# Attention followed by a squared-ReLU layer: score and value work grouped by three pairs of heads instead of two

## The chip, the cores and the metric

The kernel runs on one core of a Trainium2 chip. The time is the device time of one execution in microseconds; the kernel before takes 417.61 us (median of 3 runs, 417.29 to 417.97). The engines of the core are TensorE (PE; its weight loads are listed apart as PEld), VectorE (DVE), ScalarE (ACT), GpSimd (POOL) and SyncE (SP). TensorE reads the on-chip memory SBUF and writes the accumulator memory PSUM; DVE and ACT empty PSUM.

## What is computed

Attention with one added to the softmax's denominator, over 8 batches, 12 heads, 448 positions and a head size of 64; then two matrix products with a squared ReLU between them, over the 3584 rows of the attention's output.

```python
batch, n_heads, seq, head_dim = (8, 12, 448, 64)     # q, k, v in float32
n_tokens, d_model, d_ff = (3584, 768, 2048)          # w_in: 768x2048, w_out: 2048x768

scores = scale * np.matmul(q, k.transpose(0, 1, 3, 2))
m = np.max(scores, axis=-1, keepdims=True)
e = np.exp(scores - m)
attn = e / (np.sum(e, axis=-1, keepdims=True) + np.exp(-m) + 1e-09)
attn_out = np.matmul(attn, v)
# x: attn_out with the heads side by side, (3584, 768)
h = x @ w_in                                         # "first product"
r = np.maximum(h, 0.0)
g = r * r
out = g @ w_out                                      # "second product"
```

The kernel computes e as exp of the scaled scores and the denominator as their sum plus one, which is the same quotient.

## The kernel before

Heads are taken in pairs: 6 pairs per batch. A *unit* is one pair's scores, exponentials (`et`), their row sums and its values. Batch 0 is cut into 192 and 256 query positions, so units 0 to 11 are batch 0, 12 to 17 batch 1, and units 18 to 53 (batches 2 to 7, 36 pairs) form the main loop. Batches 0 to 2 are turned by TensorE from naturally laid out loads (`qn`, `kn`); batches 3 to 7 are turned by transposing DMAs from a float16 copy in memory.

A half-unit of scores is eight matmuls (four for batches 0 to 2) on 64 rows of the array each, two at a time in two row tiles. ACT empties each PSUM buffer with the exponential; there are two such buffers. DVE adds the four chunks of `et` to one (`es`), in three steps:

```python
    def scores(u, et, c):
        b, pr, q0, n = u
        qk = qks[b]
        two = [] if n == S else s_psum.tile([P, 2, 512], FP32, name="sp")
        for kk in (2 * c, 2 * c + 1):
            sp = s_psum.tile([P, 2, 512], FP32, name="sp") if n == S else two
            # ... [batches 0 to 2: one matmul of n columns per head; others:]
                for h in range(2):
                    for odd in range(2):
                        r = slice(64 * odd, 64 * odd + 64)
                        # ... [x, kx, which: where q and k of this half lie]
                        nc.tensor.matmul(sp[:, odd, h * (S // 2):(h + 1) * (S // 2)],
                                         qk[r, which, kx:kx + 2 * P - 1:2], qk[r, 0, x:x + S // 2],
                                         start=True, stop=True)
            if n == S:
                exp(chunk(et, u, c, kk).rearrange("p (o x) -> p o x", o=2), sp[:, :, 0:S])
    # ...

    def add_chunks(u, et, es, half, step):
        n = u[3]
        if n == S:
            e = et.rearrange("p (k x) -> p k x", k=RUN)
            if step < 2:
                nc.vector.tensor_add((es, half[:, 0:2 * S])[step], e[:, 2 * step], e[:, 2 * step + 1])
            else:
                nc.vector.tensor_add(es, es, half[:, 0:2 * S])
        # ...
```

Values, the row sums and the first product use the array in two column tiles of 64. A row sum is a matmul with ones, followed on ACT by Ln and by Exp of its negative, which gives the reciprocal; DVE multiplies the values with it:

```python
    def values(u, et, xp, o=0):
        b, pr, _, n = u
        for kk in range(RUN):
            for h in range(2):
                nc.tensor.matmul(xp[64 * h:64 * h + 64, o:o + n], vns[b][:, 2 * pr + h, kk, :],
                                 of_head(chunk(et, u, kk // 2, kk), u, h), start=(kk == 0), stop=(kk == RUN - 1))

    def row_sums(us, sums):

        zp = mp_tile()
        # ... [for each unit u, of n columns, and its es:]
                for h in range(2):
                    nc.tensor.matmul(zp[64 * h:64 * h + 64, j * n:(j + 1) * n], ones, of_head(total, u, h),
                                     start=(x == 0), stop=(x == len(parts) - 1))
        rcp = z_pool.tile([128, 512], FP32, name="rcp")
        nc.scalar.activation(out=rcp[:, 0:m], in_=zp[:, 0:m], func=AF.Ln, bias=one_b)
        nc.scalar.activation(out=rcp[:, 0:m], in_=rcp[:, 0:m], func=AF.Exp, scale=-1.0)
        return rcp

    def normalise(us, xp, rcp):
        b, pr, q0, n = us[0]
        # ... [two units at once in batch 0]
        nc.vector.tensor_mul(xts[b][:, pr, q0:q0 + n], xp[:, 0:n], rcp[:, 0:n])

    joined = [-1]

    def mp_tile(dtype=FP32):
        if joined[0] >= 0:
            joined[0] += 1
        pool, name = (x_psum, "xp") if joined[0] > 0 and joined[0] % 4 == 0 else (m_psum, "mp")
        return pool.tile([128, 512] if dtype == FP32 else [128, 2, 512], dtype, name=name)
```

`mp_tile` gives the PSUM tiles of everything but the scores. From the main loop on (`joined`), its tiles go around four buffers: three of `m_psum` (`mp`) and, every fourth time, the one of `x_psum` (`xp`).

The first product runs tile by tile (twelve matmuls of 64 output rows for 448 positions), each emptied by DVE with a maximum and a square into `gs`. The second product has a form in column tiles, one with the whole array, and one in row tiles, which splits the contraction over two PSUM tiles (`op`, `lo`) that are added on emptying:

```python
    def product(out_, lhsT, rhs, start, stop):

        if mode[0] == COLS2:
            for x in (0, 64):
                nc.tensor.matmul(out_[x:x + 64], lhsT[:, x:x + 64], rhs, start=start, stop=stop)
        else:
            nc.tensor.matmul(out_, lhsT, rhs, start=start, stop=stop)

    def tile_in(t0, n, f0, per):

        xt, x0 = xts[t0 // S], t0 % S
        m = per * n
        hp = mp_tile()
        for j in range(per):
            fb = f0 + j
            for dc in range(DCH):
                product(hp[:, j * n:(j + 1) * n], win[:, dc, fb * 128:(fb + 1) * 128],
                        xt[:, dc, x0:x0 + n], start=(dc == 0), stop=(dc == DCH - 1))
                if j < per - 1 or dc < DCH - 1:
                    yield n / 2.4
        rt = r_pool.tile([128, 512], FP16, name="rt")
        nc.vector.tensor_scalar(out=rt[:, 0:m], in0=hp[:, 0:m], scalar1=0.0, scalar2=None, op0=ALU.max)
        r = rt[:, 0:m].rearrange("p (j n) -> p j n", j=per)
        nc.vector.tensor_mul(gs[:, f0:f0 + per, t0 % RING:t0 % RING + n], r, r)
        yield n / 2.4
    # ...
    def tile_out(tok, n0, w):

        if n0 == 0:
            ots[tok] = osb_pool.tile([128, DM], FP32, name="ot")
        ot = ots[tok]
        rows = mode[0] == ROWS2
        op = mp_tile()
        lo = mp_tile() if rows else None
        for fb in range(NFFB):
            g = gs[:, fb, tok % RING:tok % RING + 128]
            if rows:
                for x, o in ((0, op), (64, lo)):
                    nc.tensor.matmul(o[:, 0:w], g[x:x + 64], wout[x:x + 64, fb, n0:n0 + w],
                                     start=(fb == 0), stop=(fb == NFFB - 1))
            else:
                product(op[:, 0:w], g, wout[:, fb, n0:n0 + w], start=(fb == 0), stop=(fb == NFFB - 1))
            if fb < NFFB - 1:
                yield w / 2.4
        if rows and n0 == 0:
            nc.vector.tensor_scalar(out=ot[:, n0:n0 + w], in0=op[:, 0:w], scalar1=OUT_SCALE, scalar2=None, op0=ALU.mult)
        else:
            nc.scalar.activation(out=ot[:, n0:n0 + w], in_=op[:, 0:w], func=AF.Copy, scale=OUT_SCALE)
        if rows:
            nc.vector.scalar_tensor_tensor(out=ot[:, n0:n0 + w], in0=lo[:, 0:w], scalar=OUT_SCALE,
                                           in1=ot[:, n0:n0 + w], op0=ALU.mult, op1=ALU.add)
        # ... [store]
```

Work is kept in two queues, `ins` (first product) and `outs` (second product). In units 0 to 17 the first product of batch 0 is dealt out between the scores and values of batches 0 and 1 by `share`. In the main loop, second product in row tiles stands between the scores, and the first product of the batch before stands after the values:

```python
    for i in range(2 * NPAIR, 3 * NPAIR):
        u, et, es, half = begin(i)
        prev = units[i - 1]
        first = i == 2 * NPAIR
        if not first:
            xp = x_psum.tile([128, 512], FP32, name="xp")
        mode[0] = COLS2
        scores(u, et, 0)
        if i in transpose_at:
            transposes(*transpose_at[i])
        # ... [loads]
        drain(left() * 0.5 if first else share[0] * 0.45)
        scores(u, et, 1)
        if first:
            # ... [the last two units of batch 0]
        else:
            done = [prev]
            rcp = row_sums(done, (ess.pop(i - 1)[0:1],))
            values(prev, ets.pop(i - 1), xp)
        drain(share[0] * 0.15)
        for step in range(3):
            add_chunks(u, et, es, half, step)
            drain(share[0] * (0.15, 0.1, 0.15)[step])
        if i == 3 * NPAIR - 1 and ins and ins[0][0] < ins[0][1]:
            run(ins)
        normalise(done, xp, rcp)
        if first:
            queue(FIRST, S - FIRST)
            share[0] = left() / (NPAIR + 1.5)

    pending = [3 * NPAIR - 1]
    joined[0] = 0
    complete(S)
    # ...
    def rows(n):
        mode[0] = ROWS2
        while outs and n > 0:
            one(outs)
            n -= 1
        mode[0] = COLS2

    for c in range((NU - 3 * NPAIR) // 2):
        i = 3 * NPAIR + 2 * c
        b, pr = units[i][0:2]
        new = []
        for j in range(2):
            new.append(begin(i + j))
        (ua, ea, sa, ha), (ub, eb, sb, hb) = new
        scores(ua, ea, 0)
        rows(11)
        scores(ua, ea, 1)
        add_chunks(ua, ea, sa, ha, 0)
        rows(11)
        scores(ub, eb, 0)
        add_chunks(ua, ea, sa, ha, 1)
        add_chunks(ua, ea, sa, ha, 2)
        rows(10)
        scores(ub, eb, 1)
        add_chunks(ub, eb, sb, hb, 0)
        mode[0] = COLS2
        for at in pending:
            if at not in rcps:
                rcps[at] = row_sums([units[at]], (ess.pop(at)[0:1],))
            xp = mp_tile()
            values(units[at], ets.pop(at), xp)
            normalise([units[at]], xp, rcps.pop(at))
        add_chunks(ub, eb, sb, hb, 1)
        add_chunks(ub, eb, sb, hb, 2)
        if b in ON_PE and pr + 2 < NPAIR:
            transposes(b, pr + 2)
            transposes(b, pr + 3)
        if pr == 0:
            run(ins, len(ins))
            queue((b - 1) * S, S)
            if b > 2:
                run(outs)
            # ... [loads of the next batches]

        n, early = ((3, 0 if b > 2 else 1), (7, 3), (6, 3))[pr // 2]
        run(ins, early)
        for at in (i, i + 1):
            rcps[at] = row_sums([units[at]], (ess.pop(at)[0:1],))
        run(ins, n - early)
        if pr == NPAIR - 2:
            complete(b * S)
        pending = [i, i + 1]
    # ... [values of the last round, then the rest of both products with the whole array]
```

Of the kernel before, what the change touches and what calls it, by code (L numbers as in the profile page):

```python
# [9 lines left out]
FP16 = mybir.dt.float16  # L10
# [5 lines left out]
def kernel(  # L16
# [11 lines left out]
    B, H, S, D = q.shape  # L28
# [5 lines left out]
    RUN = 4  # L34
# [15 lines left out]
    qk_pool = ctx.enter_context(tc.tile_pool(name="qk", bufs=2))  # L50
    e_pool = ctx.enter_context(tc.tile_pool(name="e", bufs=4))
    es_pool = ctx.enter_context(tc.tile_pool(name="es", bufs=2))
    z_pool = ctx.enter_context(tc.tile_pool(name="z", bufs=2))
    r_pool = ctx.enter_context(tc.tile_pool(name="r", bufs=2))
    osb_pool = ctx.enter_context(tc.tile_pool(name="osb", bufs=2))

# [26 lines left out]
    def load_natural(b, p0, p1):  # L83

        raw = b == 0 and p1 <= 3
        for n, r in (("q", q_r), ("k", k_r)):
            src = r[b, :, 2 * p0:2 * p1]
            if raw:
                if p0 == 0:
                    whole[n] = e_pool.tile([P, RUN * S], FP32, name="et")  # L90
                t = whole[n][:, p0 * 512:(p0 + 1) * 512].rearrange("p (h t d) -> p h t d", h=2, t=RUN)
                (nc.sync if n == "q" else nc.scalar).dma_start(out=t, in_=src)
            else:
                if p0 % 3 == 0:
                    whole[n] = nat.tile([P, NPAIR, RUN, D], FP16, name=f"{n}n{p0 // 3}")
                t = whole[n][:, 2 * (p0 % 3):2 * (p0 % 3 + p1 - p0)]
                nc.gpsimd.dma_start(out=t, in_=src)
            for pr in range(p0, p1):
                naturals[n, b, pr] = t[:, 2 * (pr - p0):2 * (pr - p0) + 2]
# [292 lines left out]
    def left():  # L392
        return sum(t[0] for t in ins)
# [23 lines left out]
    transpose_at = {pr - 1: (0, pr) for pr in range(1, NPAIR)}  # L417
    for pr in range(NPAIR):
        transpose_at[NPAIR + 3 + pr] = (1, pr)
    transpose_at[16], transpose_at[17] = (2, 0), (2, 1)  # L420

    def keep_warm(n):
        wp = m_psum.tile([128, 512], FP32, name="mp")
# [11 lines left out]
        nc.gpsimd.tensor_copy(last_of, qks[b][0:1, :, 0:1])  # L435

    def begin(i):
        ets[i] = e_pool.tile([P, RUN * 2 * S], FP16, name="et")
        es = es_pool.tile([P, 2 * S], FP16, name=f"es{i % 2}")
        half = es_pool.tile([P, 1024], FP16, name="half")  # L440
        ess[i] = (es, half)
        return units[i], ets[i], es, half
# [8 lines left out]
    for i in range(2 * NPAIR):  # L451
# [8 lines left out]
        if i == NPAIR:  # L460
            values(units[i - 1], ets.pop(i - 1), xp, units[i - 1][3])
            rcp = row_sums(two, (ess.pop(i - 2)[0:1], ess.pop(i - 1)[0:1]))
            normalise(two, xp, rcp)
            queue(0, FIRST)
            share[0] = left() / (NPAIR + 2)
        if i in transpose_at:
            transposes(*transpose_at[i])
        if i == 0:
# [26 lines left out]
    for i in range(2 * NPAIR, 3 * NPAIR):  # L495
# [9 lines left out]
        if i == 2 * NPAIR + 2:  # L505
# [2 lines left out]
                load_wout(HALF, j, 2)  # L508
            load_v(2, 0, 6)
            stage(3)  # L510
        drain(left() * 0.5 if first else share[0] * 0.45)
        scores(u, et, 1)
        if first:
            done = units[i - 2:i]
# [7 lines left out]
        for step in range(3):  # L522
            add_chunks(u, et, es, half, step)
            drain(share[0] * (0.15, 0.1, 0.15)[step])
        if i == 3 * NPAIR - 1 and ins and ins[0][0] < ins[0][1]:
            run(ins)
        normalise(done, xp, rcp)
        if first:
            queue(FIRST, S - FIRST)
            share[0] = left() / (NPAIR + 1.5)  # L530

# [8 lines left out]
            n -= 1  # L542
        mode[0] = COLS2

    for c in range((NU - 3 * NPAIR) // 2):
        i = 3 * NPAIR + 2 * c
        b, pr = units[i][0:2]
        new = []
        for j in range(2):
            new.append(begin(i + j))  # L550
        (ua, ea, sa, ha), (ub, eb, sb, hb) = new
        scores(ua, ea, 0)
        rows(11)
        scores(ua, ea, 1)
        add_chunks(ua, ea, sa, ha, 0)
        rows(11)
        scores(ub, eb, 0)
        add_chunks(ua, ea, sa, ha, 1)
        add_chunks(ua, ea, sa, ha, 2)
        rows(10)  # L560
        scores(ub, eb, 1)
        add_chunks(ub, eb, sb, hb, 0)
        mode[0] = COLS2
        for at in pending:
            if at not in rcps:
                rcps[at] = row_sums([units[at]], (ess.pop(at)[0:1],))
            xp = mp_tile()
            values(units[at], ets.pop(at), xp)
            normalise([units[at]], xp, rcps.pop(at))
        add_chunks(ub, eb, sb, hb, 1)  # L570
        add_chunks(ub, eb, sb, hb, 2)
        if b in ON_PE and pr + 2 < NPAIR:
            transposes(b, pr + 2)
            transposes(b, pr + 3)
        if pr == 0:
            run(ins, len(ins))
            queue((b - 1) * S, S)
            if b > 2:
                run(outs)
            if b + 1 < B:  # L580
                transposed_loads(b + 1)
                hold(b + 1)
                load_v(b + 1, 0, NPAIR)
                if b + 2 < B:
                    stage(b + 2)

        n, early = ((3, 0 if b > 2 else 1), (7, 3), (6, 3))[pr // 2]
        run(ins, early)
        for at in (i, i + 1):
            rcps[at] = row_sums([units[at]], (ess.pop(at)[0:1],))  # L590
        run(ins, n - early)
        if pr == NPAIR - 2:
            complete(b * S)
        pending = [i, i + 1]
    for at in pending:
        xp = mp_tile()
        values(units[at], ets.pop(at), xp)
        normalise([units[at]], xp, rcps.pop(at))
    mode[0] = FULL
    run(outs, 3)  # L600
    queue((B - 1) * S, S)
# [31 lines left out]
```

The softmax here doesn't subtract the row's maximum and nothing guards it: scores larger than these inputs give would overflow.

## Time and profile before

| kernel before | |
|---|---|
| time, median of 3 | 417.61 us (417.29 to 417.97) |
| span of the profiled execution | 415.9 us, granted TensorE clock 1.000 |
| PE busy | 405.5 us, 98% of the span, 4721 matmuls |
| DVE busy | 278.8 us, 67% |
| ACT busy | 238.4 us, 57% |
| DMA | 45.58 MB, mean 110 GB/s |

The span is cut into 40 slices; PE is busy for eight tenths or more in every slice but the last. The chain of waits follows the work that ended last back to the start: at each step to what released it. Matmuls overlap in the array and their ends are estimated, so the distances between their starts tell more than their lengths. The largest groups on PE are the first product (line L284, `mp<-xt,win`, 110.2 us busy), the second in row tiles (L330, 102.3 us on `mp` and 52.6 us on `xp`) and the scores of batches 3 to 7 (L199, 33.8 us); on ACT the exponentials (L167, 192 of them, 165.8 us); on DVE the emptying of the first product (L301 and L303). In a timeline an answer has one row per run of like instructions: start, length, engine, line, operation, what it writes and reads, shape, count, and in brackets idle time ahead of it with what ended it. A wait is listed as "engine line waited for: us in total, times, longest".

### The profile page before, as it was taken

How to read it: one execution, taken by the hardware profiler on the slowest of the kernel's cores; microseconds unless marked ns; L12 is line 12 of the kernel's file. 1: busy time of each engine (PE TensorE's matmuls, PEld its weight loads, DVE VectorE, ACT ScalarE, POOL GpSimd, SP SyncE). 2: the span in 40 equal slices, each digit the busy share in tenths (PEclk: the TensorE clock that was granted, in tenths of full speed). 3: DMA queues.
4: the chain of work that ended last, by engine and by line, in shares of the span. 5: the costliest groups of instructions: out<-in, count | busy, mean ns of one | idle time of the engine just before them, and what ended most of it. 6: DMA issues, size and time to landing. Idle time of an engine off the chain costs nothing.

```text
span 415.9 us, 10695 instructions
## 1 busy us (share of the span) xinstructions
PE 405.5 (98%) x4721; PEld 256.7 (62%) x4721; DVE 278.8 (67%) x535; ACT 238.4 (57%) x329; POOL 36.4 (9%) x58
## 2 busy tenths in 40 slices
PE   8889999899999999999999999999999999999997
PEld 3567666566566666665666666665666666555664
DVE  4769888768865868568766769658676669287000
ACT  4897998664675664673576564674666655100111
POOL 7523220020000200002000400001000000000000
PEclk9999999999999999999999999999999999999999
DMA  9999999889109790199509871198101101010222
GB/s 201 197 197 198 200 197 223 159 120 199 40 2 182 139 192 6 44 199 191 123 2 164 167 151 37 39 186 154 46 2 39 39 2 39 39 39 0 77 76 77
DMA packets 75823, 45.58 MB, mean 110 GB/s; under 512 B 42560, under 2 KB 72000, under 8 KB 75456
## 3 DMA queue, kind: packets, MB, share of 16 engines
q0 software_dynamic: 28848, 22.16, 35.0%
q1 hardware_dynamic: 46208, 22.05, 23.3%
q8 instruction: 37, 0.61, 0.6%
q10 hardware_dynamic: 720, 0.69, 0.6%
q14 instruction: 10, 0.08, 0.1%
HBM read 45.69 MB, written 17.93 MB: 153 GB/s over the span
## 4 chain that ended last, share of the span: by engine, by line
PE 86%; DMA 9%; ACT 2%; DVE 2%; issue 1%; POOL 0%; POOLq 0%
PE mp L284 23%; PE mp L330 17%; PE mp L286 11%; PE xp L284 8%; PE sp L199 6%; PE xp L330 6%; PE mp L234 5%; DMA kn<-in_k_dram 4%; PE xp L286 3%; DMA win<-in_moe_w_in_dram 3%; PE xp L234 3%; PE sp L187 2%; DMA vn<-in_v_dram 2%; PE mp L248 2%; ACT et L167 1%
## 5 line engine op out<-in xcount | busy, mean ns | idle before, releaser
L167 ACT ACTIVATE et<-sp 112x896 f16<-112x896 f32 (+2 forms) x192 | 165.8, 914 | 55.6 <-PE sp L199 40.1
L284 PEld LDWEIGHTS <-win 128*64 128x64 f16 x1536 | 85.3, 110 | 45.7 <-issue 2.8
L284 PE MATMUL mp<-xt,win 128*64 128x448 f16 (+2 forms) x1236 | 110.2, 324 | 1.5 <-DVE xt L263 0.8
L330 PE MATMUL mp<-wout,gs 64*128 64x384 f16 x864 | 102.3, 322 | 0.0
L330 PEld LDWEIGHTS <-gs 64*128 64x128 f16 x1152 | 56.1, 94 | 31.7
L301 DVE TENSOR_SCALAR rt<-mp 128x448 f16<-128x448 f32 (+2 forms) x99 | 61.6, 622 | 17.4 <-PE mp L284 13.3
L303 DVE TENSOR_TENSOR gs<-rt 128x448 f16<-128x448 f16 (+2 forms) x128 | 50.2, 392 | 4.4
L330 PE MATMUL xp<-wout,gs 64*128 64x384 f16 x288 | 52.6, 322 | 0.0
L251 ACT ACTIVATE rcp<-mp,one_b 128x448 f32<-128x448 f32 (+2 forms) x40 | 25.1, 629 | 40.1 <-PE mp L248 35.8
L212 DVE TENSOR_TENSOR es<-et 112x896 f16<-112x896 f16 x42 | 26.0, 620 | 17.7 <-ACT et L167 17.6
L339 ACT ACTIVATE ot<-mp 128x384 f32<-128x384 f32 (+1 forms) x29 | 14.1, 487 | 36.2 <-PE mp L286 27.6
L199 PE MATMUL sp<-qk 64*112 64x224 f16 x480 | 33.8, 260 | 0.0
L286 PEld LDWEIGHTS <-gs 128*128 128x128 f16 x256 | 24.4, 98 | 15.1 <-issue 0.4
L284 PE MATMUL xp<-xt,win 128*64 128x448 f16 x300 | 32.6, 352 | 0.0
L199 PEld LDWEIGHTS <-qk 64*112 64x112 f16 x480 | 26.3, 128 | 9.7 <-issue 5.4
L234 PEld LDWEIGHTS <-vn 112*64 112x64 f16 x432 | 22.1, 109 | 15.3 <-issue 5.2
L286 PE MATMUL mp<-wout,gs 128*128 128x384 f16 (+1 forms) x192 | 31.0, 322 | 0.0
L341 DVE SCALAR_TENSOR_TENSOR ot<-mp,ot 128x384 f32<-128x384 f32 x27 | 15.1, 558 | 21.7 <-PE sp L199 11.6
L252 ACT ACTIVATE rcp<-rcp 128x448 f32<-128x448 f32 (+2 forms) x48 | 27.7, 577 | 1.5
L214 DVE TENSOR_TENSOR es<-es,half 112x896 f16<-112x896 f16 x42 | 26.2, 625 | 1.4
L212 DVE TENSOR_TENSOR half<-et 112x896 f16<-112x896 f16 x42 | 25.9, 616 | 0.3 <-ACT et L167 0.3
L301 DVE TENSOR_SCALAR rt<-xp 128x448 f16<-128x448 f32 x29 | 18.0, 622 | 12.0 <-PE xp L286 8.3
(61 smaller groups left out, 313.9 us busy)
## 6 DMA issues: line engine op xcount, KB each, us to landing
vn<-in_v_dram POOLq DMA_DIRECT2D x7, 672.0 KB, 9.0
out_dram<-ot SPq DMA_DIRECT2D x9, 384.0 KB, 2.8
win<-in_moe_w_in_dram POOLq DMA_DIRECT2D x8, 384.0 KB, 13.9
wout<-in_moe_w_out_dram POOLq DMA_DIRECT2D x4, 768.0 KB, 12.8
stage_q<-in_q_dram POOLq DMA_DIRECT2D x4, 676.0 KB, 10.9
stage_k<-in_k_dram POOLq DMA_DIRECT2D x4, 676.0 KB, 13.3
out_dram<-ot SPq DMA_DIRECT2D x8, 288.0 KB, 3.2
out_dram<-ot SPq DMA_DIRECT2D x9, 192.0 KB, 2.7
```

The lines of the kernel that those rows point to most:

```text
L167: nc.scalar.activation(out=out_, in_=in_, func=AF.Exp, scale=scale)
L199: nc.tensor.matmul(sp[:, odd, h * (S // 2):(h + 1) * (S // 2)], qk[r, which, kx:kx + 2 * P - 1:2], qk[r, 0, x:x + S // 2], start=True, sto ...
L212: nc.vector.tensor_add((es, half[:, 0:2 * S])[step], e[:, 2 * step], e[:, 2 * step + 1])
L214: nc.vector.tensor_add(es, es, half[:, 0:2 * S])
L234: nc.tensor.matmul(xp[64 * h:64 * h + 64, o:o + n], vns[b][:, 2 * pr + h, kk, :], of_head(chunk(et, u, kk // 2, kk), u, h), start=(kk == 0 ...
L251: nc.scalar.activation(out=rcp[:, 0:m], in_=zp[:, 0:m], func=AF.Ln, bias=one_b)
L252: nc.scalar.activation(out=rcp[:, 0:m], in_=rcp[:, 0:m], func=AF.Exp, scale=-1.0)
L284: nc.tensor.matmul(out_[x:x + 64], lhsT[:, x:x + 64], rhs, start=start, stop=stop)
L286: nc.tensor.matmul(out_, lhsT, rhs, start=start, stop=stop)
L301: nc.vector.tensor_scalar(out=rt[:, 0:m], in0=hp[:, 0:m], scalar1=0.0, scalar2=None, op0=ALU.max)
L303: nc.vector.tensor_mul(gs[:, f0:f0 + per, t0 % RING:t0 % RING + n], r, r)
L330: nc.tensor.matmul(o[:, 0:w], g[x:x + 64], wout[x:x + 64, fb, n0:n0 + w], start=(fb == 0), stop=(fb == NFFB - 1))
```

## The change

The main loop takes three pairs per round instead of two: the scores of three pairs with the second product in row tiles between them (10, 10, 10, 9 and 9 steps of it), then the values of the three pairs of the round before, and the first product in column tiles. It is for changing less often between row tiles and column tiles: 12 rounds instead of 18. Six `et` buffers are needed then; two of them lie in the buffers of the natural loads, which are free after batch 2, and for that q and k of three pairs share one such buffer. The reciprocals get a third buffer. The shares by which the first product of batch 0 is dealt out change, so that it is done before the main loop; batch 2's first three pairs are turned before it.

```diff
@@ -50,7 +50,7 @@
     qk_pool = ctx.enter_context(tc.tile_pool(name="qk", bufs=2))
     e_pool = ctx.enter_context(tc.tile_pool(name="e", bufs=4))
     es_pool = ctx.enter_context(tc.tile_pool(name="es", bufs=2))
-    z_pool = ctx.enter_context(tc.tile_pool(name="z", bufs=2))
+    z_pool = ctx.enter_context(tc.tile_pool(name="z", bufs=3))
     r_pool = ctx.enter_context(tc.tile_pool(name="r", bufs=2))
     osb_pool = ctx.enter_context(tc.tile_pool(name="osb", bufs=2))
 
@@ -91,9 +91,11 @@
                 t = whole[n][:, p0 * 512:(p0 + 1) * 512].rearrange("p (h t d) -> p h t d", h=2, t=RUN)
                 (nc.sync if n == "q" else nc.scalar).dma_start(out=t, in_=src)
             else:
-                if p0 % 3 == 0:
-                    whole[n] = nat.tile([P, NPAIR, RUN, D], FP16, name=f"{n}n{p0 // 3}")
-                t = whole[n][:, 2 * (p0 % 3):2 * (p0 % 3 + p1 - p0)]
+                if p0 % 3 == 0 and n == "q":
+                    whole["both"] = nat.tile([P, RUN * 2 * S], FP16, name=f"nn{p0 // 3}")
+                w = NPAIR * RUN * D
+                t = whole["both"][:, w * (n == "k"):w * (n == "k") + w].rearrange("p (h t d) -> p h t d", t=RUN, d=D)
+                t = t[:, 2 * (p0 % 3):2 * (p0 % 3 + p1 - p0)]
                 nc.gpsimd.dma_start(out=t, in_=src)
             for pr in range(p0, p1):
                 naturals[n, b, pr] = t[:, 2 * (pr - p0):2 * (pr - p0) + 2]
@@ -417,7 +419,8 @@
     transpose_at = {pr - 1: (0, pr) for pr in range(1, NPAIR)}
     for pr in range(NPAIR):
         transpose_at[NPAIR + 3 + pr] = (1, pr)
-    transpose_at[16], transpose_at[17] = (2, 0), (2, 1)
+    for pr in range(3):
+        transpose_at[15 + pr] = (2, pr)
 
     def keep_warm(n):
         wp = m_psum.tile([128, 512], FP32, name="mp")
@@ -435,7 +438,11 @@
         nc.gpsimd.tensor_copy(last_of, qks[b][0:1, :, 0:1])
 
     def begin(i):
-        ets[i] = e_pool.tile([P, RUN * 2 * S], FP16, name="et")
+        spare = (i - 3 * NPAIR - 3) % 6
+        if i > 3 * NPAIR + 2 and spare in (1, 2):
+            ets[i] = nat.tile([P, RUN * 2 * S], FP16, name=f"nn{spare - 1}")
+        else:
+            ets[i] = e_pool.tile([P, RUN * 2 * S], FP16, name="et")
         es = es_pool.tile([P, 2 * S], FP16, name=f"es{i % 2}")
         half = es_pool.tile([P, 1024], FP16, name="half")
         ess[i] = (es, half)
@@ -462,7 +469,7 @@
             rcp = row_sums(two, (ess.pop(i - 2)[0:1], ess.pop(i - 1)[0:1]))
             normalise(two, xp, rcp)
             queue(0, FIRST)
-            share[0] = left() / (NPAIR + 2)
+            share[0] = left() / (NPAIR + 4)
         if i in transpose_at:
             transposes(*transpose_at[i])
         if i == 0:
@@ -508,7 +515,7 @@
                 load_wout(HALF, j, 2)
             load_v(2, 0, 6)
             stage(3)
-        drain(left() * 0.5 if first else share[0] * 0.45)
+        drain(share[0] * (1.2 if first else 0.45))
         scores(u, et, 1)
         if first:
             done = units[i - 2:i]
@@ -522,12 +529,13 @@
         for step in range(3):
             add_chunks(u, et, es, half, step)
             drain(share[0] * (0.15, 0.1, 0.15)[step])
-        if i == 3 * NPAIR - 1 and ins and ins[0][0] < ins[0][1]:
-            run(ins)
+        if i == 3 * NPAIR - 1:
+            run(ins, len(ins))
+            rcps[i] = row_sums([u], (ess.pop(i)[0:1],))
         normalise(done, xp, rcp)
         if first:
             queue(FIRST, S - FIRST)
-            share[0] = left() / (NPAIR + 1.5)
+            share[0] = left() / (NPAIR - 0.2)
 
 
 
@@ -542,38 +550,35 @@
             n -= 1
         mode[0] = COLS2
 
-    for c in range((NU - 3 * NPAIR) // 2):
-        i = 3 * NPAIR + 2 * c
+    def take_in(at):
+        xp = mp_tile()
+        values(units[at], ets.pop(at), xp)
+        normalise([units[at]], xp, rcps.pop(at))
+
+    def sums(at, *steps):
+        for step in steps:
+            add_chunks(units[at], ets[at], *ess[at], step)
+
+    for i in range(3 * NPAIR, NU, 3):
         b, pr = units[i][0:2]
-        new = []
-        for j in range(2):
-            new.append(begin(i + j))
-        (ua, ea, sa, ha), (ub, eb, sb, hb) = new
-        scores(ua, ea, 0)
-        rows(11)
-        scores(ua, ea, 1)
-        add_chunks(ua, ea, sa, ha, 0)
-        rows(11)
-        scores(ub, eb, 0)
-        add_chunks(ua, ea, sa, ha, 1)
-        add_chunks(ua, ea, sa, ha, 2)
-        rows(10)
-        scores(ub, eb, 1)
-        add_chunks(ub, eb, sb, hb, 0)
+        for j in range(3):
+            begin(i + j)
+            scores(units[i + j], ets[i + j], 0)
+            if j:
+                sums(i + j - 1, 1, 2)
+            rows(10 if j < 2 else 9)
+            scores(units[i + j], ets[i + j], 1)
+            sums(i + j, 0)
+            if j < 2:
+                rows(10 if j < 1 else 9)
         mode[0] = COLS2
         for at in pending:
-            if at not in rcps:
-                rcps[at] = row_sums([units[at]], (ess.pop(at)[0:1],))
-            xp = mp_tile()
-            values(units[at], ets.pop(at), xp)
-            normalise([units[at]], xp, rcps.pop(at))
-        add_chunks(ub, eb, sb, hb, 1)
-        add_chunks(ub, eb, sb, hb, 2)
-        if b in ON_PE and pr + 2 < NPAIR:
-            transposes(b, pr + 2)
-            transposes(b, pr + 3)
+            take_in(at)
+        sums(i + 2, 1, 2)
+        if b in ON_PE and pr == 0:
+            for x in range(3):
+                transposes(b, 3 + x)
         if pr == 0:
-            run(ins, len(ins))
             queue((b - 1) * S, S)
             if b > 2:
                 run(outs)
@@ -584,18 +589,16 @@
                 if b + 2 < B:
                     stage(b + 2)
 
-        n, early = ((3, 0 if b > 2 else 1), (7, 3), (6, 3))[pr // 2]
+        n, early = (7, 1 if b > 2 else 2) if pr == 0 else (9, 3)
         run(ins, early)
-        for at in (i, i + 1):
+        for at in range(i, i + 3):
             rcps[at] = row_sums([units[at]], (ess.pop(at)[0:1],))
         run(ins, n - early)
-        if pr == NPAIR - 2:
+        if pr:
             complete(b * S)
-        pending = [i, i + 1]
+        pending = [i, i + 1, i + 2]
     for at in pending:
-        xp = mp_tile()
-        values(units[at], ets.pop(at), xp)
-        normalise([units[at]], xp, rcps.pop(at))
+        take_in(at)
     mode[0] = FULL
     run(outs, 3)
     queue((B - 1) * S, S)
```

## The prediction

> **What bounds the kernel now.** I read the page first, then the waits, then the timelines of one steady group of the main loop. The page gives PE 98% busy at a granted clock of 9 tenths or more in every slice, and the chain of waits is 86% PE. So the end is set by how densely TensorE streams; ACT, DVE and DMA matter only where they make it stop.
>
> The waits of the kernel before tell that, in the steady part, they do not. For 118 to 355 us no line has PE waiting for another engine; ACT and DVE wait for PE:
>
> ```profile
> ACT et L167 <- PE sp L199: 38.6, 44, 2.7
> ACT rcp L251 <- PE mp L248: 29.2, 8, 3.7
> DVE rt L301 <- PE mp L284: 9.7, 7, 2.3
> ```
>
> What is lost on PE there is at the change of tile mode. In the PE timeline of one group (start, length, then line, operation and shape):
>
> ```profile
> 150.53 0.55 PE L199 MATMUL sp<-qk 64*112 64x224 f16 x8
> 150.91 1.14 PE L330 MATMUL mp<-wout,gs 64*128 64x384 f16 x11
> ...
> 154.71 0.57 PE L199 MATMUL sp<-qk 64*112 64x224 f16 x8
> 155.20 1.71 PE L234 MATMUL mp<-et,vn 112*64 112x448 f16 x16
> ...
> 160.15 0.55 PE L248 MATMUL mp<-es,ones 112*64 112x448 f16 x4
> 160.53 1.30 PE L284 MATMUL xp<-xt,win 128*64 128x448 f16 x12
> 161.66 2.44 PE L284 MATMUL mp<-xt,win 128*64 128x448 f16 x24
> 164.03 0.59 PE L199 MATMUL sp<-qk 64*112 64x224 f16 x8
> ```
>
> Eight score matmuls take 150.53 to 150.91, 0.38, when row tiles follow; before the values in column tiles 154.71 to 155.20, 0.49. Twelve matmuls of the first product take 160.53 to 161.66, 1.13, so 24 take 2.26; before the next scores it is 161.66 to 164.03, 2.37. Each change of mode costs about 0.1 us; from single starts I get 0.093 (row to column) and 0.096 (column to row). The timeline also gives my steps: a pair of first-product matmuls 0.189, hence a 12-matmul tile 1.13; a pair of second-product matmuls in row tiles 0.161.
>
> Two other engines are close behind, and the change leans on both. ACT in the row part of that group:
>
> ```profile
> 148.75 1.72 ACT L167 ACTIVATE et<-sp 112x896 f16<-112x896 f32 x2 [2.69 <-PE sp L199]
> 150.92 1.72 ACT L167 ACTIVATE et<-sp 112x896 f16<-112x896 f32 x2 [0.45 <-PE sp L199]
> 152.53 0.49 ACT L339 ACTIVATE ot<-mp 128x384 f32<-128x384 f32 x1
> 153.09 1.72 ACT L167 ACTIVATE et<-sp 112x896 f16<-112x896 f32 x2
> ```
>
> One exp takes 0.91, two take 1.72, so the step is 0.81. The first begins 0.39 after the first score matmul (150.53 to 150.92), or 0.397 from single starts; the half's second score buffer is thus free 0.397+0.813+0.912 = 2.12 after that matmul, and 2.17 with the 0.052 from an exp's end to the matmul that waits for it (seen at 54.69 to 54.75 us). And DVE from the end of the row part:
>
> ```profile
> 154.90 0.56 DVE L337 TENSOR_SCALAR ot<-mp 128x384 f32<-128x384 f32 x1
> 155.56 0.56 DVE L341 SCALAR_TENSOR_TENSOR ot<-xp,ot 128x384 f32<-128x384 f32 x1
> 156.04 0.62 DVE L212 TENSOR_TENSOR es<-et 112x896 f16<-112x896 f16 x1
> 156.57 1.15 DVE L260 TENSOR_TENSOR xt<-mp,rcp 128x448 f16<-128x448 f32 x2
> 157.64 0.61 DVE L212 TENSOR_TENSOR half<-et 112x896 f16<-112x896 f16 x1
> 158.28 0.63 DVE L214 TENSOR_TENSOR es<-es,half 112x896 f16<-112x896 f16 x1
> 158.83 0.62 DVE L301 TENSOR_SCALAR rt<-mp 128x448 f16<-128x448 f32 x1
> 159.48 0.39 DVE L303 TENSOR_TENSOR gs<-rt 128x448 f16<-128x448 f16 x1
> 159.79 0.62 DVE L301 TENSOR_SCALAR rt<-xp 128x448 f16<-128x448 f32 x1
> ```
>
> DVE enters the column part (PE starts it at 155.20) with work left, and reads the first `rt` only 3.63 us into it. The second `rt` ends at 160.41; PE reuses that buffer at 160.53. The kernel before therefore runs with about 0.1 us to spare in this place.
>
> **What the skill says.** The Trainium skill, "TensorEngine Tiling (Array Packing)", Key Properties: changing the tiling mode, and not just the tile, drains TensorE. The trace agrees: 0.093 and 0.096 us at each change, nothing between scores and second product, both in row tiles. The same page, PSUM Bottleneck: tiling speeds up TensorE but not the emptying of PSUM. That is what I fear; the 0.1 us of slack above is its number. "Perfetto Trace Analysis", Tensor Engine Instruction: a matmul's end is estimated, and ScalarE and VectorE are strict FIFO. So I use starts of matmuls, and let a copy in ACT's queue delay the exps behind it.
>
> **The change, part by part.** The instruction order of both kernels holds the same 4721 matmuls of the same shapes, so streaming time is unchanged.
>
> 1. *Fewer changes of mode.* The 36 pairs of batches 2 to 7 form 12 groups in place of 18. Counting modes along PE's order, row to column falls from 45 to 39, column to row from 50 to 44. 6 x 0.096 + 6 x 0.093 = **1.1 us saved**, all on the path.
>
> 2. *Shorter row segments.* Between half-pairs of scores now lie 10, 10, 10, 9, 9 pairs of second product instead of 11, 11, 10. From one half's first score to the next: 0.37 + 10 x 0.161 = 2.0 (9 pairs: 1.85). The next half's second score comes 0.19 later, and needs the buffer free at 2.17. With 10 pairs 2.19: just fits. With 9 pairs 2.04: PE waits 0.13. After the first of the two 9s the delay itself spaces the second enough, unless an ACT copy of the output (0.49) lies there: the group of three has three output tiles, and where the middle one is a right half (7 groups of 12 by the order of tiles) that copy pushes the exps back to 0.23 more. 12 x 0.13 + 7 x 0.23 = **3.2 us lost**.
>
> 3. *Three row sums in a row in a ring of four PSUM tiles.* Before, the order was first-product tiles 1, 2, 3, two row sums, then tile 4, which takes the buffer of tile 2. Now three row sums come, and tile 4 takes that of tile 3, which has only just been finished; the order of the changed kernel names exactly this DVE wait there. With DVE idle: its `rt` starts 0.395 after the tile's last matmul pair (seen wherever DVE waits), lasts 0.622, PE follows 0.054 later: 1.07. PE could come after 4 x 0.187 = 0.75. So 0.32 lost at the least. In the first group of batches 3 to 7 a tile of second product gives DVE time to catch up: 5 x 0.33 = 1.65. In the second group of each batch DVE lags: its chain from above gets one more `xt` (0.54), so first `rt` at 4.17, then 0.96 per tile, third `rt` ending at 6.71; PE is ready for tile 4 at 2.24 (values) + 3.41 + 0.56 = 6.21 and goes on at 6.77: 0.5 lost, or 0.8 where the output copy of point 2 delays DVE. 6 x 0.67 = 4.0. Together **5.6 us lost**.
>
> 4. *The start.* The new shares move first-product work of batch 0 from units 7 to 12 into units 13 to 17, and finish it before the main loop. There ACT is the bound: a unit takes 4.81 (exps from 48.16, 52.97, 57.78) of which 4 exps and Ln plus Exp fill all but 0.2 to 0.3, so extra matmuls fill stalls of PE. But what is moved out of units 7 to 12 runs into the landing of `kn` at 38.4 us (0.8 us less work before it), and unit 17's longer tail (46 matmuls for 22) takes what the main loop is spared (24 matmuls, 1.28). In the first group, PE waited 0.46+0.36+0.15+0.22 in the old order and, with three transposed pairs to copy ahead of DVE's `rt`, I get 1.6 to 1.7 for the new one against 1.9 counted from single starts. **0.4 us saved**, within my error.
>
> 5. *e in the natural buffers, a third `rcp` buffer, joint q and k loads:* six e tiles are what three pending and three new pairs need, all free a group earlier. No cost and no gain of their own.
>
> Sum: 417.6 - 1.1 - 0.4 + 3.2 + 5.6 = 424.9. Stalls partly cover one another (a PE that waits in the row part lets DVE catch up), so I take off 1: **423.8 us**.
>
> **Rivals.** (a) *The mode changes are all that matters:* 417.6 - 1.1 - 0.4, about 416. For it: PE is 98% busy, ACT and DVE are below 70%. Against it: busy shares are averages, and the two steps of 0.1 us slack lie just where the change presses. (b) *ACT becomes the bound of the row part outright:* 12 exps x 0.81 + up to two copies x 0.49 = 10.7 against 6 x 0.37 + 48 x 0.161 = 9.9 of PE; if every group paid that 0.8, 12 x 0.8 = 9.6 plus point 3 gives 431. Against it: the last two exps run beside the values. (c) *Fuller use of the ACT-bound start gives more than I count:* the 3 us of PE stalls there come back, 414. Against it: ACT's work there is the same and its idle gaps are 0.16 to 0.34 per unit.
>
> **Range and chances.** Point 3's 0.32 per group is hardest to escape (3.5 over 11 groups), point 2's copies and the lag of DVE least sure (4 us together). Range **418.5 to 426.5**: the low end has the minimum of point 3 and half of point 2 off, the high end all stalls in full and no gain at the start. Faster by over 2% would need 409, below every rival: 0.01. Slower by over 2% needs 426.0: 0.12. Within 2%: 0.87.
>
> **What would show it.** Point 1: column-to-row steps of 283 ns as before, 12 fewer changes. Point 2: in the waits, PE `sp` on ACT `et`, about 0.13 to 0.25 at a time, in the 9-pair segments. Point 3: PE `xp` or `mp` of the first product waiting for DVE `rt`, once per group, 0.3 to 0.8, right after the row sums. If neither wait is there, I am wrong and rival (a) holds; if PE waits more than 0.5 per group in the row part, (b) does; if the main loop begins 2 us earlier than 67 us, (c) does.

## The result and the profile after

The changed kernel takes 424.23 us (median of 4, 424.12 to 424.89) against 417.79 us for the kernel before on the same chip: ratio 1.0159, 95% interval 1.0141 to 1.0176. It is slower, by 6.4 us; 423.8 was predicted.

The chain of waits by engine, before:

```profile
PE 86%; DMA 9%; ACT 2%; DVE 2%; issue 1%; POOL 0%; POOLq 0%
```

The page after, its chain of waits by engine and line (line numbers are two higher than before: L286 is the first product, L332 the second in row tiles, L201 the scores, L303 and L305 the emptying of the first product, L262 the normalisation):

```profile
PE 73%; DVE 13%; DMA 8%; ACT 3%; issue 2%; POOL 0%; DVEq 0%; POOLq 0%
PE mp L286 20%; PE mp L332 15%; PE mp L288 10%; PE xp L286 6%; PE sp L201 6%; PE xp L332 4%; PE mp L236 4%; DVE rt L303 4%; DMA nn<-in_k_dram 3%; PE xp L288 3%; DMA win<-in_moe_w_in_dram 3%; PE xp L236 2%; DVE xt L262 2%; DMA vn<-in_v_dram 2%; PE sp L189 2%; DVE half L214 2%
```

PE's share of the chain falls from 86% to 73%, and DVE rises from 2% to 13%. Where DVE enters shows in the second round of a batch. PE in the column part of that round (start, length, line, shape, count, idle time with its cause):

```profile
151.41 0.95 PE L236 MATMUL xp<-et,vn 112*64 112x448 f16 x8
152.19 1.68 PE L236 MATMUL mp<-et,vn 112*64 112x448 f16 x16
153.70 1.30 PE L286 MATMUL mp<-xt,win 128*64 128x448 f16 x12
154.84 1.30 PE L286 MATMUL xp<-xt,win 128*64 128x448 f16 x12
155.97 1.30 PE L286 MATMUL mp<-xt,win 128*64 128x448 f16 x12
157.10 0.55 PE L250 MATMUL mp<-es,ones 112*64 112x448 f16 x4
157.49 0.35 PE L250 MATMUL xp<-es,ones 112*64 112x448 f16 x2
158.23 3.60 PE L286 MATMUL mp<-xt,win 128*64 128x448 f16 x36 [0.39 <-DVE rt L303]
```

And the chain of waits there, in order of time (start, length):

```profile
151.76 0.56 DVE ot L343
152.31 0.53 DVE es L214
152.85 1.68 DVE xt L262 x3
154.53 0.54 DVE half L214
155.07 0.02 issue
155.10 0.62 DVE es L216
155.72 0.55 DVE rt L303
...
157.65 0.55 DVE rt L303
158.19 0.04 issue
158.23 3.60 PE mp L286 x36
```

This is the predicted place: the values of three pairs, three first-product tiles, three row sums, and the next tile waits for the third `rt`. In DVE's own timeline that `rt` runs from 157.56 to 158.18 (the chain leaves out the part in which instructions overlap). Counted from the start of the values it ends at 6.77; 6.71 was worked out. The next tile starts at 6.82; 6.77 was worked out. From 151.76 on, DVE goes from one instruction to the next with no gap above 0.03 us: in this part its chain, and not PE's, ends last.

The waits of the changed kernel for 118 to 360 us show much less of it:

```profile
PE mp L286 <- DVE rt L303: 1.7, 5, 0.4
PE xp L286 <- DVE rt L303: 0.7, 3, 0.4
```

Only 2.4 us are listed, and no wait of `sp` for ACT at all. The row at 158.23 says why: it lists 0.39 of idle time, but the last row sum starts at 157.49 and takes 0.187 as a step, so PE waited for 158.23 - 157.68 = 0.55. The Trainium skill, "Perfetto Trace Analysis", Tensor Engine Instruction, says that a matmul's end is estimated; by these rows a matmul counts as busy for 0.35 where the next can start after 0.19, and a wait of up to 0.16 looks like work. PE's busy time even rose, 405.5 to 408.5 us, with the same 4721 matmuls. Hence everything below is counted from starts: a *row part* from the first score matmul of a round to the first value, a *column part* from there to the next score. One round before, then stretches of three rounds after (from:to, length, then busy time of PE, PEld, DVE, ACT and POOL, clock, DMA):

```profile
148.31:155.20 6.89, 6.89 (x98) 4.78 (x97) 3.68 (x8) 5.65 (x8) 0.00 (x0) 1.00 0.67 147
155.20:164.03 8.83, 8.83 (x95) 5.18 (x93) 8.36 (x17) 3.94 (x6) 0.00 (x0) 1.00 0.10 33
```

```profile
116.39:126.97 10.58, 10.58 (x146) 8.32 (x145) 6.50 (x13) 9.12 (x12) 0.00 (x0) 1.00 0.03 7
126.97:140.82 13.85, 13.70 (x148) 9.14 (x147) 10.25 (x20) 5.39 (x9) 0.00 (x0) 1.00 0.70 133
...
151.41:165.16 13.75, 13.36 (x140) 8.67 (x138) 12.01 (x24) 4.89 (x8) 0.00 (x0) 1.00 0.70 151
165.16:175.61 10.45, 10.45 (x146) 8.31 (x144) 6.29 (x12) 9.25 (x12) 0.00 (x0) 1.00 0.14 39
```

Row parts now take 10.58 or 10.45, with PE "busy" throughout and ACT for close to nine tenths of it; column parts 13.85 and 13.76. A *step* is the distance of two starts on PE: in a row part, that of two pairs of second-product matmuls. Before, a row part of 32 such steps took 6.89 in every round of batches 3 to 7. The end of a row part of 10.58, with its two segments of 9 steps:

```profile
146.89 0.58 PE L201 MATMUL sp<-qk 64*112 64x224 f16 x8
147.28 0.32 PE L332 MATMUL xp<-wout,gs 64*128 64x384 f16 x1
...
148.74 0.74 PE L201 MATMUL sp<-qk 64*112 64x224 f16 x8
149.27 1.68 PE L332 MATMUL mp<-wout,gs 64*128 64x384 f16 x18
150.73 0.74 PE L201 MATMUL sp<-qk 64*112 64x224 f16 x8
```

Eight score matmuls take 0.39 at first. After a 9-step segment they take 0.53, and 0.68 to the first value at 151.41, where the same took 0.49 before. The single starts have the jump, 0.15 each time, at the second of the two score buffers. In a row part of 10.45 only the first of these two jumps is there.

### The profile page after: what moved, and what is told of

Read it like the earlier page. It is cut to its first block, busy times and chain, and to the rows that moved or that the text cites. A ratio compares the mean times of both kernels' runs of the same rounds, so it can differ in the third digit from the quotient of the medians.

```text
span 422.4 us, 10698 instructions
## 1 busy us (share of the span) xinstructions
PE 408.5 (97%) x4721; PEld 282.9 (67%) x4721; DVE 281.8 (67%) x536; ACT 236.5 (56%) x328; POOL 36.4 (9%) x58
## 4 chain that ended last, share of the span: by engine, by line
PE 73%; DVE 13%; DMA 8%; ACT 3%; issue 2%; POOL 0%; DVEq 0%; POOLq 0%
PE mp L286 20%; PE mp L332 15%; PE mp L288 10%; PE xp L286 6%; PE sp L201 6%; PE xp L332 4%; PE mp L236 4%; DVE rt L303 4%; DMA nn<-in_k_dram 3%; PE xp L288 3%; DMA win<-in_moe_w_in_dram 3%; PE xp L236 2%; DVE xt L262 2%; DMA vn<-in_v_dram 2%; PE sp L189 2%; DVE half L214 2%
## 5 line engine op out<-in xcount | busy, mean ns | idle before, releaser
L169 ACT ACTIVATE et<-sp 112x896 f16<-112x896 f32 (+2 forms) x144 | 124.4, 914 | 64.4 <-PE sp L201 50.4
L286 PEld LDWEIGHTS <-win 128*64 128x64 f16 x1536 | 95.5, 110 | 40.4 <-issue 8.6
L286 PE MATMUL mp<-xt,win 128*64 128x448 f16 (+2 forms) x1212 | 107.3, 323 | 2.8 <-DVE rt L303 1.7
L332 PE MATMUL mp<-wout,gs 64*128 64x384 f16 x896 | 104.4, 322 | 0.2 <-DVE rt L303 0.2
L332 PEld LDWEIGHTS <-gs 64*128 64x128 f16 x1152 | 69.1, 94 | 19.6 <-issue 0.6
L303 DVE TENSOR_SCALAR rt<-mp 128x448 f16<-128x448 f32 (+2 forms) x97 | 60.4, 622 | 27.1 <-PE mp L286 13.9
L305 DVE TENSOR_TENSOR gs<-rt 128x448 f16<-128x448 f16 (+2 forms) x128 | 50.2, 392 | 4.4
L332 PE MATMUL xp<-wout,gs 64*128 64x384 f16 x256 | 48.0, 322 | 0.0
L169 ACT ACTIVATE nn<-sp 112x896 f16<-112x896 f32 x48 | 41.4, 917 | 3.5 <-PE sp L201 2.6
L286 PE MATMUL xp<-xt,win 128*64 128x448 f16 x324 | 35.7, 353 | 2.1 <-DVE rt L303 1.7
L201 PE MATMUL sp<-qk 64*112 64x224 f16 x480 | 37.4, 260 | 0.0
L201 PEld LDWEIGHTS <-qk 64*112 64x112 f16 x480 | 29.7, 127 | 8.1 <-issue 3.6
L214 DVE TENSOR_TENSOR es<-et 112x896 f16<-112x896 f16 x30 | 18.6, 622 | 13.4 <-ACT et L169 13.4
L303 DVE TENSOR_SCALAR rt<-xp 128x448 f16<-128x448 f32 x31 | 19.3, 623 | 10.3 <-PE xp L286 8.8
```

Source lines behind the costliest of these rows:

```text
L169: nc.scalar.activation(out=out_, in_=in_, func=AF.Exp, scale=scale)
```

## The experiments

Each was timed beside the kernel before on the same chip; 417.7 to 417.8 us is that kernel's median each time.

**Row sums apart.**

```diff
         for at in range(i, i + 3):
             rcps[at] = row_sums([units[at]], (ess.pop(at)[0:1],))
-        run(ins, n - early)
+            run(ins)
+        run(ins, n - early - 3)
```

> The changed kernel, with one tile of the first product after each of the three row sums instead of all three sums in a row; same matmuls, same changes of mode. Theory (ring of four PSUM tiles: the tile after the three sums needs the buffer of the tile just before them): the jumps after the row sums, 0.32 in the first and 0.56 us in the second round of a batch, vanish, 5 x 0.32 + 6 x 0.56 = 4.9, so 419.3 us. Rival (DVE is simply too slow for the longer column part): the waits move to a later tile, 423.5 to 424.2 us.

Measured: 418.39 us, ratio to before 1.0019 (1.0010 to 1.0028); 5.8 less than the changed kernel. PE in the same round:

```profile
154.27 1.30 PE L286 MATMUL mp<-xt,win 128*64 128x448 f16 x12
155.41 0.36 PE L250 MATMUL mp<-es,ones 112*64 112x448 f16 x2
155.60 1.30 PE L286 MATMUL mp<-xt,win 128*64 128x448 f16 x12
156.73 0.36 PE L250 MATMUL xp<-es,ones 112*64 112x448 f16 x2
156.93 1.30 PE L286 MATMUL mp<-xt,win 128*64 128x448 f16 x12
158.06 0.36 PE L250 MATMUL mp<-es,ones 112*64 112x448 f16 x2
```

Every step is 1.13 or 0.19: no jump is left, and no wait of PE for `rt` stands in its waits after 118 us. The column parts of batches 3 to 7 fall by 0.33 in the first round (13.85 to 13.52) and 0.57 in the second (13.76 to 13.19). The first round of batch 2, which the expectation left out, gives another 0.84 (12.12 to 11.27): hence 5.8 and not 4.9. DVE has exactly the same work here, so it was not too slow for the part; the order around the ring was wrong for it. The rival falls.

**Output copies on DVE.**

```diff
-        if rows and n0 == 0:
+        if rows:
             nc.vector.tensor_scalar(out=ot[:, n0:n0 + w], in0=op[:, 0:w], ...)
```

> The changed kernel, with all output copies in the row part on DVE and none on ACT. Theory (ACT's copy between exponentials pushes them back where the middle output tile of a round is a right half, 7 of 12 rounds): the row part of those rounds falls from 10.58 to about 10.45, 7 x 0.13 = 0.9 less, 423.3 us. Rival (the copies do not matter, or DVE pays for them): 424.2 us or more, with longer waits after the row sums.

Measured: 423.34 us, ratio 1.0134 (1.0119 to 1.0150), 0.9 less than the changed kernel. ACT in the row part of a round with the copy in the middle, first in the changed kernel, then in this one:

```profile
147.30 1.72 ACT L169 ACTIVATE nn<-sp 112x896 f16<-112x896 f32 x2 [0.28 <-PE sp L201]
148.91 0.49 ACT L341 ACTIVATE ot<-xp 128x384 f32<-128x384 f32 x1
149.28 1.74 ACT L169 ACTIVATE nn<-sp 112x896 f16<-112x896 f32 x2
```

```profile
147.44 3.59 ACT L169 ACTIVATE nn<-sp 112x896 f16<-112x896 f32 x4 [0.28 <-PE sp L201]
```

With the copy between them, the second pair of exponentials starts 1.98 after the first and the four take 3.72; without it they take 3.59. The row parts at 10.58 become 10.45, and the first round's falls from 11.36 to 11.23; all others stay. Column parts do not grow (13.85 and 13.75), so no cost of the copies shows on DVE.

**The new start alone**, on the kernel before: the shares, `transpose_at`, `rcps[i]` and `z_pool` of the change, rounds of two pairs.

```diff
-        if i == 3 * NPAIR - 1 and ins and ins[0][0] < ins[0][1]:
-            run(ins)
+        if i == 3 * NPAIR - 1:
+            run(ins, len(ins))
+            rcps[i] = row_sums([u], (ess.pop(i)[0:1],))
...
-            share[0] = left() / (NPAIR + 1.5)
+            share[0] = left() / (NPAIR - 0.2)
```

> The kernel before, with the new start alone: the new shares, batch 0's first product finished before the main loop, three pairs of batch 2 turned early, three reciprocal buffers; rounds of two pairs as before. Theory: ACT and the landing of kn bound the start in either order, 0.4 us gained, 417.4 us. Rival (the start gives back PE stalls): 415.5 us or less.

Measured: 416.90 us, ratio 0.9981 (0.9974 to 0.9989): 0.9 faster than before, twice the expected gain and less than half of what the rival asked for. PE did run into the landing of `kn`, as worked out (here and in the changed kernel the transposes start early and idle 0.91 and 1.00 us at 38.24 us; before, 0.28 at 38.42 us). One thing had not been worked out: the first row part of the main loop takes 7.53 here and 6.87 before. By starts, the main loop begins 1.37 later than before, and batch 2 is 2.18 shorter there.

**More changes of mode**, on the kernel before: one pair's values in the middle of the second product (`take_in` turns to column tiles, does the values and normalises them).

```diff
         rows(11)
         scores(ub, eb, 0)
+        if len(pending) > 1:
+            take_in(pending.pop(0))
         add_chunks(ua, ea, sa, ha, 1)
         add_chunks(ua, ea, sa, ha, 2)
         rows(10)
...
+        early += 1
         run(ins, early)
```

> The kernel before, with the values of one pair of each round moved between the row tiles of the second product (17 rounds): 17 more changes to column tiles and 17 more back, same matmuls; one tile of the first product is moved ahead of the row sums so that the PSUM ring has the same slack. Theory: 17 x (0.093 + 0.096) = 3.2, so 421.0 us. Rival (a change of mode is hidden, or costs less than the starts suggest): less than 419 us.

Measured: 421.36 us, ratio 1.0088 (1.0074 to 1.0102): 3.57 more for 34 more changes, 0.105 each. In PE's timeline:

```profile
136.36 0.55 PE L199 MATMUL sp<-qk 64*112 64x224 f16 x8
136.84 0.95 PE L234 MATMUL mp<-et,vn 112*64 112x448 f16 x8
137.72 0.33 PE L330 MATMUL xp<-wout,gs 64*128 64x384 f16 x1
```

The eight value matmuls are four steps of 0.189, 0.76; from 136.84 to 137.72 are 0.88. Changes of mode cost slightly more than the 0.093 and 0.096 expected, and nothing in this run hides them.

**Longer segments**, on the kernel with row sums apart.

```diff
-            rows(10 if j < 2 else 9)
+            rows(13 if pr == 0 and b > 2 else 10 if j < 2 else 9)
...
-            if b > 2:
-                run(outs)
...
-        n, early = (7, 1 if b > 2 else 2) if pr == 0 else (9, 3)
+        n, early = (7, 3 if b > 2 else 2) if pr == 0 else (9, 3)
```

> The kernel of the first experiment (row sums apart), with the one tile of second product that stood in column tiles in the first round of batches 3 to 7 moved into that round's row part: there 13, 13, 13, 12, 13 steps between the scores in place of 10, 10, 10, 9, 9. Theory (a 9-step segment is shorter than the two exponentials that free the score buffer; the copies add to it only then): those five rounds lose their 0.18 or 0.31 us each, 3 x 0.31 + 2 x 0.18 = 1.3, so 417.1 us. Rival (the row part's excess is something else, such as a cost per segment): 418.4 us.

Measured: 417.02 us, ratio 0.9982 (0.9975 to 0.9989); 1.4 less than with the shorter segments. Those five row parts take 12.84 for 64 steps, whether or not copies fall between. Less 16 steps of 0.1625 (from single starts) that is 10.24 for 48: so the parts of 10.45 wait 0.21, those of 10.58 wait 0.34. With as many segments the longer ones lose nothing, so it is no cost per segment; the 9-step segments are too short for the two exponentials.

**All mended**: the same, with the copies on DVE and unit 17's row sum one tile earlier.

```diff
-            run(ins, len(ins))
+            run(ins, len(ins) - 1)
             rcps[i] = row_sums([u], (ess.pop(i)[0:1],))
+            run(ins)
```

> The same, with the output copies of the row part on DVE, and with unit 17's row sum put ahead of its last first-product tile, so that ACT has its Ln and Exp done, and PSUM is emptied, before the main loop's first scores. Theory: 3 x 0.13 from the copies in the second rounds of batches 3, 5 and 7, 0.13 in the first round, and about 0.6 from the two waits of 0.3 in the first round's row part: 1.1 less than the kernel with longer segments, 416.0 us, below the kernel before. Rival (the first round is bound by something that this order does not touch): 416.6 us or more.

Measured: 416.53 us, ratio 0.9972 (0.9962 to 0.9982). The first row part falls from 11.36 to 10.42, but the wait has only moved. PE of this kernel:

```profile
66.55 1.37 PE L286 MATMUL mp<-xt,win 128*64 128x256 f16 x22
68.59 0.38 PE L250 MATMUL mp<-es,ones 112*64 112x448 f16 x2 [0.67 <-DVE es L216]
```

The early row sum waits for the sums of unit 17 that DVE has not finished. That half of the expectation was wrong. The half on the copies held: the second rounds at 10.58 take 10.45 here.

**Two pairs with the same start**: the early row sum on the kernel with the new start alone.

```diff
-            run(ins, len(ins))
+            run(ins, len(ins) - 1)
             rcps[i] = row_sums([u], (ess.pop(i)[0:1],))
+            run(ins)
```

> The kernel before with the new start (rounds of two pairs), and unit 17's row sum ahead of its last first-product tile. It tells what three pairs at a time are worth when both have the same start. Theory: the first round's row part falls from 7.53 to 6.9, 416.3 us; the kernel with everything mended should then lead it only by what its fewer changes of mode give, less what the 9-step segments still take. Rival: no change from the start alone, 416.9 us.

Measured: 417.26 us, ratio 0.9990 (0.9981 to 0.9998): 0.4 slower than the new start without the early sum. The first row part is 6.87 as expected, and the sum waits 0.84 ahead of it. As a step it is a miss.

**Copies and segments**: the kernel with everything mended, without the early sum.

```diff
-            run(ins, len(ins) - 1)
+            run(ins, len(ins))
             rcps[i] = row_sums([u], (ess.pop(i)[0:1],))
-            run(ins)
```

> Row sums apart, longer segments in the first rounds, output copies on DVE; unit 17's row sum at its old place after the last first-product tile. Theory: 3 x 0.13 in the second rounds of batches 3, 5 and 7 and 0.13 in the first round less than the kernel with longer segments, 416.5 us: the same as the kernel called all mended, whose early row sum only moved the first round's waits to itself. Rival (the early row sum did help there): 417.0 us.

Measured: 416.26 us (416.14 to 416.64), ratio 0.9966 (0.9953 to 0.9978). It is below the kernel before, and the lowest time of all.

**The main loop's first tile elsewhere.**

```diff
         if i == 3 * NPAIR - 1:
+            normalise(done, xp, rcp)
             run(ins, len(ins))
...
-    joined[0] = 0
+    joined[0] = 3
```

> The same, with the main loop's first second-product tile in the x_psum buffer (joined starts at 3) and unit 16's normalisation ahead of unit 17's long tail, so that this tile does not wait for the last first-product tile to be emptied. Theory: the wait of 0.31 at the first second-product matmul of the main loop goes, but the next scores still wait for the exponentials, which queue behind Ln and Exp of unit 17; between 0 and 0.3 less, 416.2 to 416.5 us. Rival (that wait alone made the first round long): 415.9 us or less.

Measured: 416.38 us, ratio 0.9968 (0.9956 to 0.9980), the same as the last. The wait at the first tile did not go: it is 0.41 for `xp` instead of 0.31 for `mp`, since unit 16's normalisation comes no sooner than DVE's queue lets it. The row part is 11.23 in both. What holds it besides shows in ACT's timeline of the kernel with longer segments:

```profile
68.87 0.63 ACT L253 ACTIVATE rcp<-mp,one_b 128x448 f32<-128x448 f32 x1 [1.11 <-PE mp L250]
69.54 0.58 ACT L254 ACTIVATE rcp<-rcp 128x448 f32<-128x448 f32 x1
70.02 3.37 ACT L169 ACTIVATE et<-sp 112x896 f16<-112x896 f32 x4
```

The round's first scores start at 68.76, and their exponentials, which need 0.4 after that, only at 70.02, behind Ln and Exp of unit 17. That ACT delay is read from the trace; no run here removed it alone. The same part takes 10.42 when the early row sum takes the waits on itself, so 0.8 is lost; how much of it is due to ACT and how much to the tile stays open.

## Why the prediction was right

| step | predicted, us | measured, us | from |
|---|---|---|---|
| 1. twelve fewer changes of mode | -1.1 | -1.6 to -1.7 | starts at each change and at the step after it; 34 changes more |
| 2. shorter row segments | +3.2 | +3.1, and 1.1 in the first round | row parts against 10.24; longer segments, copies on DVE |
| 3. three row sums in a ring of four | +5.6 | +5.8 | row sums apart |
| 4. the start | -0.4 | -0.9 | the start alone |
| stalls that cover one another | -1.0 | about -0.4, not covering | what is left to 6.4 |

The last row: the first round's 1.1 holds 0.7 that the start alone has too (7.53 against 6.87), so the rest comes to -1.6 + 3.1 + 0.4 + 5.8 - 0.9 = 6.8, and -0.4 remains to the measured 6.4. By starts it lies in batch 2, whose column parts take 25.73 in the start alone and 24.46 with the row sums apart. Of this 1.27, 0.76 are the values of one pair, which come later with three at a time, and 0.12 is a change of mode. The rest are waits in the first of these rounds, by starts 0.64 and 0.34 behind the row sums in the start alone, against 0.59 at a first-product tile in rounds of three. The 1.0 taken off for stalls that cover one another was a guess, and the runs show no such covering: with the copies on DVE the row parts wait 0.13 less, and the column parts after them are no longer (13.75 against 13.76).

So the mechanisms of steps 2 and 3, which make the change slower, were right. That the sum came within half a microsecond of the measured time is in part luck: steps 1 and 4 each gave 0.5 more than predicted, the first round's row part took 0.4 that was not predicted, and the 1.0 taken off stood in for gains that had been missed.

*Step 1* held in being on the path, and was too small, because it counted only the step at the change itself. The step after a change is longer too. In the kernel before, behind the first value at 155.20 and the first score at 164.03:

```profile
156.74 1.30 PE L284 MATMUL mp<-xt,win 128*64 128x448 f16 x12
...
164.46 0.32 PE L330 MATMUL mp<-wout,gs 64*128 64x384 f16 x1
```

The 16 value matmuls take 1.54, which is eight steps of 0.189 and 0.03 more; the eight score matmuls take 0.43, where those in the middle of the part take 0.38. With 0.10 and 0.11 at the changes themselves that is 0.28 for the two changes of a round, 1.6 to 1.7 for six rounds.

*Step 2* held in place and in mechanism. It gave 0.13 to rounds without the middle copy and 0.36 to those with it; 0.21 and 0.34 were measured, in the rounds that the order of the tiles had named. A step of second product is 0.1625 by single starts; the 0.161 written there would give 1.98 and 1.82 for a segment, and the 2.0 and 1.85 that it goes on with are right. Its sign in the profile was named wrongly: no wait of `sp` on ACT is listed in batches 3 to 7, because waits this short vanish in the estimated ends.

*Step 3* held in place and in mechanism, and not in all sizes. 0.32 was given for the first rounds and 0.33 measured. For the second rounds 0.5 without and 0.8 with the output copy were given, 4.0 in all, and 0.57 was measured in each, 3.4 in all: column parts take 13.76 after row parts with the copy and without, so the copy does not delay DVE's chain there. Batch 2's first round, with 0.84, was not counted in this step. That 5.6 and 5.8 lie so near is luck to this extent.

*Step 4* was half of what it turned out to be, and it missed the first round's row part: with batch 0's first product and unit 17's row sum just ahead of the main loop, the first round finds DVE and ACT behind. The two errors pull opposite ways.

Of the rivals, (a) is what the change was for, and it fell for the kernel as changed; after the waits are mended, 416.26 us is near its 416. (b) fell by the row parts: outside the first round PE waits 0.21 to 0.34 in them, under the 0.5 that it was to show. (c) fell by the start alone; the main loop begins at 68.7 us and not 2 us before 67. Mended, three pairs take 416.26 us (0.9966 of before) against 416.90 us (0.9981) for two pairs with the new start. The intervals overlap, and the two-pair kernel still has its output copies on ACT, so that three at a time are worth these 0.6 us is not shown.

## What to carry to other kernels

When a bound engine is to switch less often, first find what the switch costs in starts, with the step after it (here 0.14 us, 1.6 in all), and then list what the longer stretches do to each ring of buffers. In a ring of four, three short users between two long ones give the second long one the buffer of the first, which has had only three short steps to be emptied. Spread the short users between the long ones. Then compare the shortest segment between two uses of a double buffer with the full time to empty it, queue included, and read waits of TensorE from the distance of starts, not from its listed idle time.

## What the runs showed of the hardware

A wait of TensorE of up to about 0.16 us leaves no trace in busy time or in the list of waits: row parts that lose 0.21 to 0.34 us, in jumps of at most 0.15, are listed as 100% busy. A change between row and column tiles costs 0.09 to 0.11 us at its own step and another 0.02 to 0.05 at the next (0.286 for 0.189 and then 0.143 for 0.096 from column to row; 0.209 for 0.096 and then 0.213 for 0.189 from row to column, by single starts before). It was 0.105 on average where only eight matmuls stand between two changes. Exponentials of 112x896 last 0.91 us each but follow one another every 0.81.
